# Sigmoid attention into a Swish MLP: v of the first heads loaded earlier, their values between the first score passes, and layer one's first pass dealt anew

## The chip, the cores and the metric

One core of a Trainium2 chip. The metric is the device time of one execution in microseconds. PE is the matmul engine, ACT the scalar engine (here: sigmoids and a few copies), DVE the vector engine (transpositions, casts, products), POOL the engine that issues the loads of inputs, SP the one that issues the first two loads and the stores.

## The reference

```python
scores = scale * np.matmul(q, k.transpose(0, 1, 3, 2)) - np.log(S)   # q, k, v: (8, 12, 448, 64)
attn = 1.0 / (1.0 + np.exp(-scores))
x = np.matmul(attn, v)          # then transposed to (8 * 448, 12 * 64) = (3584, 768)
h = x @ w_in                    # (768, 2048)
g = h * (1.0 / (1.0 + np.exp(-beta * h)))
out = g @ w_out                 # (2048, 768)
```

The attention is a sigmoid for each score, with no normalisation over a row, so scores and values of any piece can be worked on by themselves.

## The kernel before

**Groups and slots.** The 12 heads of a batch are three groups of four heads (g = 0, 1, 2 for batch 0; 3, 4, 5 for batch 1). A group has two slots of two heads. The 448 keys are three blocks of 128 and a last block of 64; the values `vs[b]` hold, for each of 128 partitions and each head, the three full blocks and one place for the last block, which `double_v_last` (step `E`) copies to the upper partitions.

**Loads.** q and k of a group come in one raw tile, turned by DVE into `qT` and `kT` (`transpose`, step `R`: `R3.1` makes kT of group 3, with two instructions, `R3.0` its qT). POOL issues all loads but the first two in the order of the program, with a cast from f32 to f16 on the way. The loads take turns on eight semaphores, so that a load is issued when the one eight before it has landed. `load_v` makes six loads: four of the full blocks (L136) and two of the last block (L143, rows of 64 elements). w_in comes in eight chunks (L153), each of which serves two of the sixteen column blocks of layer one; group 0's q and k come through SP as f32 and are cast by DVE and ACT (L747 to L750).

**The prologue.** For batch 0 the queries are split in two halves (c0 = 0 and c0 = QH = 224). `half_visit(g, c0, second)` is one score pass: 16 matmuls (L218) into two score tiles, then two sigmoids on ACT (L230); `second` 0 takes key blocks 0 and 1, `second` 1 block 2 and the last one. There are three score tiles in the first stage and two from then on, and a score tile is free when its sigmoid has read it. `attend(g, c0, n)` multiplies a group's weights with its values (16 matmuls, L291, into two banks) and DVE casts the two results into `xT` (L300). `idle_units` are matmuls on zeros (L740), fillers. Here the order is written out by hand: six score passes of the first query half with fillers between, then values and the first passes of the second half, then layer one's first half, `first_half(n)`: n units, each six matmuls (L171), a sigmoid (L317) and a product (L320) for one column block of 224 tokens. A unit of layer one for the other 224 tokens is a step `D0.x`.

**Behind it** the list `STEPS` gives the order of the rest, from `D0` on: `V3.1` is a score pass of group 3 with key block 1 (two score tiles, two sigmoids of 896), `A` values, `O`, `I` and `U` the two layers. Each engine runs its instructions in the order in which the steps stand.

Of the kernel before, what the change touches and what calls it, by code (L numbers as in the profile page):

```python
# [8 lines left out]
FP32 = mybir.dt.float32  # L9
FP16 = mybir.dt.float16  # L10
# [3 lines left out]
def kernel(  # L14
# [10 lines left out]
    nc = tc.nc  # L25
# [3 lines left out]
    B, H, S, D = q.shape  # L29
    NTOK, DM = out.shape  # L30
    DFF = moe_w_in.shape[1]
    P = 128
    BLK = 32
    HQ = P // BLK
    NB = S // BLK
    PAIR = D // BLK
    JF = S // P
    KL = S - JF * P
    NF = JF * P // BLK
    NPAIR = H // 2  # L40
    QPB = H // HQ
# [47 lines left out]
    def bank(name: str, cols: int = S, hold=None):  # L89
        i = min((i for i in used if i not in held.values()), key=used.get)  # L90
        touch(i)
        if hold is not None:
            held[hold] = i
        pool = psum["one" if i < N_ONE else "late"]
        return pool.tile([P, cols], FP32, tag=f"one{i}", name=name)
# [33 lines left out]
    def last_base(s: int) -> int:  # L129
        return (s % 2 ^ swapped(s // 2)) * KL  # L130

    def load_v(b: int):
        vs[b] = vp.tile([P, H, JF + 1, D], FP16, tag="v16", name="v16")
        rows = v[b].rearrange("h (p c) d -> p h (c d)", c=NB)
        for i in range(HQ):
            nc.gpsimd.dma_start(  # L136
                out=vs[b][i * BLK : (i + 1) * BLK, :, 0:JF].rearrange("p h j d -> p h (j d)"),
                in_=rows[:, :, JF * i * D : JF * (i + 1) * D],
            )
        rows = v[b].rearrange("h (p c) d -> p h c d", c=NB)  # L140
        for c in range(NF, NB):
            lo = (c - NF) * BLK
            nc.gpsimd.dma_start(out=vs[b][lo : lo + BLK, :, JF], in_=rows[:, :, c])  # L143

    def double_v_last(b: int):
        nc.vector.tensor_copy(out=vs[b][KL:P, :, JF], in_=vs[b][0:KL, :, JF])
# [44 lines left out]
    def transpose(g: int, r: int, c0: int = 0, c1: int = NB):  # L191
        raw = raws[g][:, r]
        if r == 0:
            if g not in qT:
                qT[g] = qTp.tile([P, NB * BLK, PAIR], FP16, tag="qT", name="qT")
            nc.vector.transpose(
                out=in_order(g // QPB, qT[g][:, c0 * BLK : c1 * BLK]),
                in_=raw[:, c0:c1].rearrange("p c d -> p (c d)").bitcast(FP32),
            )
            return  # L200
        kT[g] = kTp.tile([P, S, PAIR], FP16, tag="kT", name="kT")
        to = kT[g].rearrange("p k e -> p (k e)").bitcast(FP32)
        frm = raw.rearrange("p c d -> p (c d)").bitcast(FP32).rearrange("p (c f) -> p c f", c=NB)
        nc.vector.transpose(  # L204
            out=to[:, 0 : JF * P].rearrange("p (j i q) -> p i j q", j=JF, i=HQ),
            in_=frm[:, 0:NF].rearrange("p (i j) f -> p i j f", j=JF),
        )
        nc.vector.transpose(
            out=to[:, JF * P :], in_=frm[:, NF:].rearrange("p c f -> p (c f)")
        )  # L210
# [45 lines left out]
    def half_visit(g: int, c0: int, second: int):  # L256
        slots = (2 * g, 2 * g + 1)
        scos = [score_tile() for _ in slots]
        plan = [(s, jt, sco, jt * QH) for jt in (0, 1) for s, sco in zip(slots, scos)]
        widths = [S, S]  # L260
        if second:
            plan = [(s, 2, sco, 0) for s, sco in zip(slots, scos)]
            plan += [(s, JF, scos[0], QH) for s in slots]
            widths = [S, QH]
        for i in range(0, len(plan), 2):
            for e in range(PAIR):
                for s, jt, sco, u0 in plan[i : i + 2]:
                    for hh in range(2):
                        score(sco, u0, s, jt, hh, e, c0, QH)
        homes = [None, None]  # L270
        if c0 == 0 and g < QPB - 1:
            home = outp.tile([P, 2 * S], FP32, tag="osb", name="early")
            home = home.bitcast(FP16).rearrange("p (x h s) -> p x h s", x=2, h=2)
            homes = [home[:, x] for x in range(2)]
        ats = {id(sco): weigh(sco, n, at) for sco, n, at in zip(scos, widths, homes)}
        for s, jt, sco, u0 in plan:
            at_tiles[s, jt, c0] = ats[id(sco)][:, :, u0 : u0 + QH]
# [329 lines left out]
    def first_half(n: int):  # L607
        for _ in range(n):
            dense1(0, todo.pop(0), 0, QH)
# [28 lines left out]
    def follow(steps):  # L638
# [9 lines left out]
                scores_done()  # L648

    STEPS = """  # L650
        R3.1 R3.0 D0.6 D0.12 R4.1 D0.14 D0.7 V3.1 R4.0 D0.13 D0.0 D0.8 V3.0 D0.3 D0.9 V3.3 D0.1
        D0.10 E1 D0.2 Q6 V3.2 D0.4 O0.0.0 D0.5 O0.0.1 O0.0.2 V4.1 O1.0.0 O0.0.3 A3 V4.0 O1.0.1 R5.1
        D0.11 D0.15 O0.0.4 R5.0 V4.2 O0.0.5 S1.1 O0.0.6 O1.0.2 O1.0.3 S1.0 O0.0.7 S2.0 O1.0.4 V4.3
        O1.0.5 A4 V5.1 O1.0.6 O0.1.0 O0.1.1 O1.1.0 S2.1 Q7 T3.1 O1.0.7 S4.0 T2.1 O0.1.2 V5.0 T3.0
# [58 lines left out]
    with tc.manual_schedule():  # L713
        raws[0] = rawp.tile([P, 2, NB, D], FP16, tag="raw", name="raw")
        wide = gt.rearrange("p a b -> p (a b)").bitcast(FP32)
        cut = NH * D
        early = [(0, 0, NH), (1, 0, NB)]
        staged = {}
        at = 0
        for r, c0, c1 in early:  # L720
            staged[r] = wide[:, at : at + (c1 - c0) * D]
            at += (c1 - c0) * D
            nc.sync.dma_start(  # L723
                out=staged[r],
                in_=(q, k)[r][0, 0:HQ].rearrange("h (p c) d -> (h p) (c d)", c=NB)[
                    :, c0 * D : c1 * D
                ],
            )
        nc.gpsimd.memset(dummy, 0.0)
        nc.scalar.activation(out=dummy, in_=dummy, func=AF.Sigmoid, bias=0.0, scale=1.0)  # L730

        still = gt[:, NDC - 1, 0:512]
        nc.vector.memset(still, 0.0)
        beta_in = sigp.tile([P, S], FP32, tag="sg", name="beta_in")[0:BLK, 0:P]
        nc.vector.memset(beta_in, 0.0)
        idle = bank("idle_ps", 512)

        def idle_units(n: int, cols: int = 512):
            for _ in range(n):
                nc.tensor.matmul(  # L740
                    idle[:, 0:cols], still[:, 0:P], still[:, 0:cols], start=True, stop=True
                )

        idle_units(10)
        idle_units(1, 256)
        raw = raws[0].rearrange("p r c d -> p r (c d)")
        nc.vector.tensor_copy(out=raw[:, 0, 0:cut], in_=staged[0])  # L747
        transpose(0, 0, 0, NH)
        nc.scalar.copy(out=raw[:, 1, cut:], in_=staged[1][:, cut:])  # L749
        nc.vector.tensor_copy(out=raw[:, 1, 0:cut], in_=staged[1][:, 0:cut])  # L750
        transpose(0, 1)
        for g in range(1, QPB):
            load_one(g, 0, 0, NH)
            load_one(g, 1)
        load_v(0)
        nc.sync.dma_start(out=beta_in[0:NDC], in_=moe_beta.rearrange("(c p) -> c p", p=P))
        for g in range(QPB - 1):
            load_one(g, 0, NH, NB)
        for c in range(WCH):
            if c == WCH // 2:  # L760
                load_one(QPB - 1, 0, NH, NB)
            load_w_in(c)
        for g in range(1, QPB):
            transpose(g, 0, 0, NH)
            transpose(g, 1)

        for g in range(QPB):
            for second in range(2):
                half_visit(g, 0, second)
                if 2 * g + second < 2 * QPB - 1:  # L770
                    idle_units(4 if g < QPB - 1 else 2)
        double_v_last(0)
        transpose(0, 0, NH, NB)
        attend(0, 0, QH)
        half_visit(0, QH, 0)
        attend(1, 0, QH)
        half_visit(0, QH, 1)
        for g in range(1, QPB - 1):
            transpose(g, 0, NH, NB)
        attend(2, 0, QH, (0,))  # L780
        attend(2, 0, QH, (1,))
        for i in range(P // BLK):
            part = slice(i * BLK, (i + 1) * BLK)
            nc.vector.transpose(out=beta_sb[part], in_=beta_in[:, part])
        load_qk(QPB)
        load_qk(QPB + 1)
        load_v(1)
        load_w_out(0, 0)
        load_w_out(1, 0)
        load_qk(QPB + 2)  # L790
        load_w_out(0, 1)
        load_w_out(1, 1)

        firsts.close()
        share_psum(ctx, seconds, 2, N_ONE, 2)
        first_half(4)
        half_visit(1, QH, 0)
        first_half(3)
        half_visit(1, QH, 1)
        transpose(2, 0, NH, NB)  # L800
        attend(0, QH, QH)
        first_half(1)
        half_visit(2, QH, 0)
        first_half(4)
        half_visit(2, QH, 1)
        attend(1, QH, QH)
        first_half(3)
        attend(2, QH, QH)
        first_half(1)
        follow(STEPS)  # L810


# [28 lines left out]
```

## Time and profile before

| | us |
|---|---|
| median of 3 runs (368.26 to 369.42) | 368.48 |
| profiled execution | 368.51 |
| its span, first to last instruction | 366.7 |
| PE busy, fillers and all | 361.6 |
| ACT busy / DVE busy | 248.7 / 271.7 |
| first score pass starts / layer one starts | 6.00 / 19.42 |

A row of a timeline gives start, length, engine, line, operation, what it writes and reads, and in brackets how long the engine sat idle before it and what ended that. Matmul rows overlap by some hundredths at their ends. The profiled execution has 1.8 us around its span. The DMA engines are busy without a break from about 3 us to about 72 us, with 177 GB/s in the mean over the first 20 us.

### The profile page before, as it was taken

To read this page: it belongs to the slowest core of one execution; us is meant where nothing else is said; L and a number is where in the kernel's file an instruction comes from. 1 tells how busy PE (TensorE), PEld (TensorE's weight loads), DVE (VectorE), ACT (ScalarE), POOL (GpSimd) and SP (SyncE) were. 2 spreads that over 40 slices of the span, in tenths; PEclk is the share of its full clock that TensorE was granted. 3 is DMA by queue.
4 is the path that set the end of the run, shared out by engine and by line. 5 is a ranking of instruction groups with operands and counts; after the bars stand their busy time and mean duration, and the time that the engine had idled before them with its cause. 6 is when DMAs were issued, how large, how long until landed. Compare 5 with 4: busy or idle time off the path is not lost.

```text
span 366.7 us, 9126 instructions
## 1 busy us (share of the span) xinstructions
PE 361.6 (99%) x3677; PEld 238.0 (65%) x3677; DVE 271.7 (74%) x521; ACT 248.7 (68%) x409; POOL 154.3 (42%) x192
## 2 busy tenths in 40 slices
PE   8999999999999999999999999999999999999996
PEld 3478754457465685557857667666856687679763
DVE  3356569889995796876778678868878667678764
ACT  4987976789765797657865579977874859226410
POOL 7834523504413873117761445841630316316610
PEclk9999999999999999999999999999999999999999
DMA  8999999930363790416919363373303030030234
GB/s 168 184 197 201 199 206 198 236 39 2 50 139 52 160 152 2 74 64 111 156 13 149 52 137 52 49 81 89 52 1 89 2 88 2 0 88 0 56 68 138
DMA packets 42698, 34.76 MB, mean 95 GB/s; under 512 B 21904, under 2 KB 39200, under 8 KB 42656
## 3 DMA queue, kind: packets, MB, share of 16 engines
q0 software_dynamic: 36688, 22.47, 44.8%
q1 hardware_dynamic: 5968, 11.71, 11.5%
q8 instruction: 29, 0.48, 0.6%
q14 instruction: 13, 0.11, 0.1%
HBM read 45.62 MB, written 11.01 MB: 154 GB/s over the span
## 4 chain that ended last, share of the span: by engine, by line
PE 93%; DMA 3%; ACT 2%; DVE 1%; SPq 0%; issue 0%; ACTq 0%; DVEq 0%
PE m_ps L171 71%; PE sco L218 12%; PE av_ps L291 9%; DMA out_dram<-osb 2%; ACT attnT L230 1%; PE idle_ps L740 1%; DMA gt<-in_k_dram 1%; DVE osb L372 0%; SPq L602 0%; ACT osb L425 0%; DVE xT L300 0%; DVE kT L204 0%; ACT raw L749 0%; ACT osb L463 0%; SPq L723 0%
## 5 line engine op out<-in xcount | busy, mean ns | idle before, releaser
L230 ACT ACTIVATE attnT<-sco 128x896 f16<-128x896 f32 (+1 forms) x163 | 139.2, 908 | 37.8 <-PE sco L218 37.1
L372 DVE TENSOR_TENSOR osb<-m_ps,osb 128x448 f32<-128x448 f32 (+2 forms) x197 | 116.3, 596 | 51.1 <-PE m_ps L171 42.0
L171 PEld LDWEIGHTS <-w_in 128*128 128x128 f16 (+1 forms) x948 | 81.0, 100 | 18.8 <-issue 11.0
L171 PE MATMUL m_ps<-xT,w_in 128*128 128x224 f16 (+3 forms) x750 | 85.5, 266 | 0.3 <-ACT attnT L230 0.2
L492 POOL TENSOR_TENSOR gt<-osb,sg 128x448 f16<-128x448 f32 x26 | 29.5, 1135 | 117.8 <-ACT sg L425 107.7
L502 POOL TENSOR_TENSOR gt<-osb,sg 128x448 f16<-128x448 f32 x52 | 58.3, 1138 | 35.1 <-ACT sg L425 33.5
L425 ACT ACTIVATE sg<-osb,beta_sb 128x224 f32<-128x224 f32 (+1 forms) x104 | 54.0, 575 | 10.3 <-DVE osb L372 10.0
L171 PEld LDWEIGHTS <-sum 128*128 128x128 f16 (+1 forms) x444 | 39.9, 99 | 27.4 <-issue 3.6
L171 PEld LDWEIGHTS <-gt 128*128 128x128 f16 (+1 forms) x474 | 36.9, 102 | 25.7 <-issue 7.5
L171 PE MATMUL m_ps<-w_out,gt 128*128 128x384 f16 (+2 forms) x350 | 52.6, 324 | 0.0
L218 PE MATMUL sco<-qT,kT 32*128 32x448 f16 (+3 forms) x864 | 51.5, 340 | 0.3 <-ACT attnT L230 0.2
L171 PEld LDWEIGHTS <-w_S 128*128 128x128 f16 (+1 forms) x486 | 43.9, 99 | 7.0 <-issue 6.0
L171 PE MATMUL m_ps<-w_out,sum 128*128 128x384 f16 (+1 forms) x228 | 40.6, 327 | 0.0
L171 PE MATMUL m_ps<-w_T,sum 128*128 128x384 f16 (+1 forms) x216 | 40.3, 326 | 0.0
L300 DVE CAST xT<-av_ps 128x448 f16<-128x448 f32 (+1 forms) x54 | 28.4, 566 | 14.2 <-PE av_ps L291 14.1
L291 PE MATMUL av_ps<-attnT,v 128*64 128x448 f16 (+3 forms) x400 | 38.2, 343 | 0.0
L171 PE MATMUL m_ps<-xs,w_S 128*128 128x224 f16 (+1 forms) x330 | 36.2, 259 | 0.0
L291 PEld LDWEIGHTS <-v 128*64 128x64 f16 (+1 forms) x432 | 20.4, 108 | 17.7 <-issue 9.8
L425 ACT ACTIVATE osb<-m_ps,beta_sb 128x224 f32<-128x224 f32 x52 | 20.4, 448 | 15.4 <-PE m_ps L171 15.1
L218 PEld LDWEIGHTS <-kT 32*128 32x128 f16 (+1 forms) x864 | 13.5, 96 | 23.1 <-issue 21.5
L320 DVE TENSOR_TENSOR gt<-m_ps,sg 128x224 f16<-128x224 f32 (+1 forms) x40 | 16.6, 434 | 12.5 <-ACT sg L317 12.2
L463 ACT COPY osb<-m_ps 128x448 f32<-128x448 f32 x26 | 13.8, 535 | 17.7 <-PE m_ps L171 15.5
(50 smaller groups left out, 303.5 us busy)
## 6 DMA issues: line engine op xcount, KB each, us to landing
out_dram<-osb SPq DMA_DIRECT2D x100, 96.0 KB, 2.4
raw<-in_k_dram POOLq DMA_DIRECT2D x23, 224.0 KB, 5.7
raw<-in_q_dram POOLq DMA_DIRECT2D x21, 224.0 KB, 4.4
v<-in_v_dram POOLq DMA_DIRECT2D x32, 144.0 KB, 7.0
w_in<-in_moe_w_in_dram POOLq DMA_DIRECT2D x8, 384.0 KB, 10.3
w_out<-in_moe_w_out_dram POOLq DMA_DIRECT2D x4, 768.0 KB, 13.1
v<-in_v_dram POOLq DMA_DIRECT2D x16, 48.0 KB, 6.4
out_dram<-osb SPq DMA_DIRECT2D x4, 192.0 KB, 2.4
```

The costliest lines, as they stand in the source:

```text
L171: nc.tensor.matmul(to[c : c + step], hidden[:, c : c + step], weights, **({} if step == P else {"tile_position": (0, c)}), **flags,)
L218: nc.tensor.matmul(sco[base : base + nk, hh, u0 : u0 + n], kT[g][lo : lo + BLK, jt * P : jt * P + nk, e], qT[g][lo : lo + BLK, c0 : c0 + n ...
L230: nc.scalar.activation(out=at[:, :, 0:n], in_=sco[:, :, 0:n], func=AF.Sigmoid, bias=NEG_LOG_S, scale=MSCALE,)
L291: nc.tensor.matmul(av[hh * D : (hh + 1) * D, 0:n], vs[b][base : base + nk, 2 * (s % NPAIR) + hh, jt], at[base : base + nk, hh, 0:n], start ...
L300: nc.vector.tensor_copy(out=xTs[b][:, s % NPAIR, c0 : c0 + n], in_=av[:, 0:n])
L320: nc.vector.tensor_tensor(out=gt[:, dc, off : off + n], in0=m1[:, 0:n], in1=sg[:, 0:n], op=ALU.mult)
L372: nc.vector.tensor_tensor(out=out, in0=in0, in1=in1, op=op)
L425: nc.scalar.activation(out=out, in_=in_, func=AF.Sigmoid, bias=0.0, scale=beta_sb[:, dc : dc + 1])
L463: nc.scalar.copy(out=oa[:, 0], in_=m)
L492: nc.gpsimd.tensor_tensor(out=gt[:, 2 * d : 2 * d + 2, off : off + QH], in0=ob[:, 0], in1=sg, op=ALU.mult)
L502: nc.gpsimd.tensor_tensor(out=gt[:, dc, off : off + S].rearrange("p (h n) -> p h n", h=2), in0=oa[:, :, j], in1=sg, op=ALU.mult,)
L740: nc.tensor.matmul(idle[:, 0:cols], still[:, 0:P], still[:, 0:cols], start=True, stop=True)
```

## The change

- `load_v` is cut in two functions. For batch 0 the last block's two loads and the four loads of heads 0 to 3 are issued behind group 1's first query half and keys and ahead of group 2's; the four loads of heads 4 to 11 follow group 2's. Batch 0 has ten loads of v instead of six.
- Group 0's keys are cast and transposed block by block: ACT casts block 1 and the last one, DVE blocks 0 and 2, and DVE turns each block by itself.
- `attend(0, 0, QH)` stands between group 2's two first passes instead of two fillers; there are 16 fillers instead of 18 from the first pass on, and 9 and a half instead of 10 and a half before it. `attend(1, 0, QH)` and `attend(2, 0, QH)` move up as well, and `attend(2, ...)` is no longer cut in two.
- `first_half` goes 2, 2, 4, 2, 4, 2 instead of 4, 3, 1, 4, 3, 1 among the passes and values of the second query half.
- In `STEPS`, `R3.1 R3.0` come behind `D0.6 D0.12`, and `D0.13` comes ahead of `V3.1`.

```diff
-    def load_v(b: int):
-        vs[b] = vp.tile([P, H, JF + 1, D], FP16, tag="v16", name="v16")
-        rows = v[b].rearrange("h (p c) d -> p h (c d)", c=NB)
+    def load_v_full(b: int, h0: int, h1: int):
+        rows = v[b, h0:h1].rearrange("h (p c) d -> p h (c d)", c=NB)
...
+    def load_v_last(b: int):
         rows = v[b].rearrange("h (p c) d -> p h c d", c=NB)
...
-        R3.1 R3.0 D0.6 D0.12 R4.1 D0.14 D0.7 V3.1 R4.0 D0.13 D0.0 D0.8 V3.0 D0.3 D0.9 V3.3 D0.1
+        D0.6 D0.12 R3.1 R3.0 D0.14 D0.7 R4.1 D0.13 V3.1 R4.0 D0.0 D0.8 V3.0 D0.3 D0.9 V3.3 D0.1
...
-        idle_units(10)
+        idle_units(9)
         idle_units(1, 256)
...
-        nc.scalar.copy(out=raw[:, 1, cut:], in_=staged[1][:, cut:])
-        nc.vector.tensor_copy(out=raw[:, 1, 0:cut], in_=staged[1][:, 0:cut])
-        transpose(0, 1)
...
+        key_cast(nc.scalar.copy, 1)
+        nc.scalar.copy(out=raw[:, 1, NF * D :], in_=staged[1][:, NF * D :])
+        key_cast(nc.vector.tensor_copy, 0)
+        key_turn(0)
+        key_turn(1)
+        key_cast(nc.vector.tensor_copy, 2)
+        key_turn(2)
+        nc.vector.transpose(out=words[:, JF * P :], in_=raw[:, 1, NF * D :].bitcast(FP32))
+        vs[0] = vp.tile([P, H, JF + 1, D], FP16, tag="v16", name="v16")
         for g in range(1, QPB):
             load_one(g, 0, 0, NH)
             load_one(g, 1)
-        load_v(0)
+            if g == 1:
+                load_v_last(0)
+                load_v_full(0, 0, HQ)
+        load_v_full(0, HQ, H)
...
-        for g in range(QPB):
-            for second in range(2):
-                half_visit(g, 0, second)
-                if 2 * g + second < 2 * QPB - 1:
-                    idle_units(4 if g < QPB - 1 else 2)
         double_v_last(0)
+        for n in range(2 * QPB):
+            half_visit(n // 2, 0, n % 2)
+            if n == 2 * QPB - 2:
+                attend(0, 0, QH)
+            else:
+                idle_units((3, 4, 4, 4, 0, 1)[n])
         transpose(0, 0, NH, NB)
-        attend(0, 0, QH)
+        attend(1, 0, QH)
         half_visit(0, QH, 0)
-        attend(1, 0, QH)
+        attend(2, 0, QH)
         half_visit(0, QH, 1)
...
-        attend(2, 0, QH, (0,))
-        attend(2, 0, QH, (1,))
...
-        first_half(4)
+        first_half(2)
         half_visit(1, QH, 0)
-        first_half(3)
+        first_half(2)
         half_visit(1, QH, 1)
-        transpose(2, 0, NH, NB)
         attend(0, QH, QH)
-        first_half(1)
-        half_visit(2, QH, 0)
+        transpose(2, 0, NH, NB)
         first_half(4)
-        half_visit(2, QH, 1)
+        half_visit(2, QH, 0)
         attend(1, QH, QH)
-        first_half(3)
+        first_half(2)
+        half_visit(2, QH, 1)
+        first_half(4)
         attend(2, QH, QH)
-        first_half(1)
+        first_half(2)
         follow(STEPS)
```

More of the change, by code (lines that the diff above doesn't have):

```diff
@@ L130, in last_base @@
         return (s % 2 ^ swapped(s // 2)) * KL
-    def load_v(b: int):
-        vs[b] = vp.tile([P, H, JF + 1, D], FP16, tag="v16", name="v16")
-        rows = v[b].rearrange("h (p c) d -> p h (c d)", c=NB)
+    def load_v_full(b: int, h0: int, h1: int):
+        rows = v[b, h0:h1].rearrange("h (p c) d -> p h (c d)", c=NB)
         for i in range(HQ):
             nc.gpsimd.dma_start(
-                out=vs[b][i * BLK : (i + 1) * BLK, :, 0:JF].rearrange("p h j d -> p h (j d)"),
+                out=vs[b][i * BLK : (i + 1) * BLK, h0:h1, 0:JF].rearrange("p h j d -> p h (j d)"),
                 in_=rows[:, :, JF * i * D : JF * (i + 1) * D],
             )
+    def load_v_last(b: int):
         rows = v[b].rearrange("h (p c) d -> p h c d", c=NB)
@@ L143, in load_v @@
             nc.gpsimd.dma_start(out=vs[b][lo : lo + BLK, :, JF], in_=rows[:, :, c])
+    def load_v(b: int):
+        vs[b] = vp.tile([P, H, JF + 1, D], FP16, tag="v16", name="v16")
+        load_v_full(b, 0, H)
+        load_v_last(b)
     def double_v_last(b: int):
@@ L735 @@
         nc.vector.memset(beta_in, 0.0)
-        idle = bank("idle_ps", 512)
         def idle_units(n: int, cols: int = 512):
+            idle = bank("idle_ps", 512)
             for _ in range(n):
@@ L748, with key_cast, key_turn @@
         transpose(0, 0, 0, NH)
-        nc.scalar.copy(out=raw[:, 1, cut:], in_=staged[1][:, cut:])
-        nc.vector.tensor_copy(out=raw[:, 1, 0:cut], in_=staged[1][:, 0:cut])
-        transpose(0, 1)
+        whole = [
+            t[:, 0 : NF * D].rearrange("p (i j d) -> p i j d", j=JF, d=D)
+            for t in (staged[1], raw[:, 1])
+        ]
+        kT[0] = kTp.tile([P, S, PAIR], FP16, tag="kT", name="kT")
+        words = kT[0].rearrange("p k e -> p (k e)").bitcast(FP32)
+        def key_cast(copy, j: int):
+            copy(out=whole[1][:, :, j], in_=whole[0][:, :, j])
+        def key_turn(j: int):
+            nc.vector.transpose(
+                out=words[:, j * P : (j + 1) * P].rearrange("p (i q) -> p i q", i=HQ),
+                in_=raws[0][:, 1, 0:NF]
+                .rearrange("p c d -> p (c d)")
+                .bitcast(FP32)
+                .rearrange("p (i j q) -> p i j q", i=HQ, j=JF)[:, :, j],
+            )
+        key_cast(nc.scalar.copy, 1)
[7 more added lines that the diff above has]
+        vs[0] = vp.tile([P, H, JF + 1, D], FP16, tag="v16", name="v16")
         for g in range(1, QPB):
@@ L795 @@
         share_psum(ctx, seconds, 2, N_ONE, 2)
-        first_half(4)
-        half_visit(1, QH, 0)
-        first_half(3)
-        half_visit(1, QH, 1)
-        transpose(2, 0, NH, NB)
-        attend(0, QH, QH)
-        first_half(1)
+        first_half(2)
+        half_visit(1, QH, 0)
+        first_half(2)
+        half_visit(1, QH, 1)
+        attend(0, QH, QH)
+        transpose(2, 0, NH, NB)
+        first_half(4)
         half_visit(2, QH, 0)
+        attend(1, QH, QH)
+        first_half(2)
+        half_visit(2, QH, 1)
         first_half(4)
-        half_visit(2, QH, 1)
-        attend(1, QH, QH)
-        first_half(3)
         attend(2, QH, QH)
-        first_half(1)
+        first_half(2)
         follow(STEPS)
```

## The prediction

> **What bounds the kernel now.** I read the page first (busy shares, the slices, the chain), then PE's timeline of the first 45 us, then ACT's and DVE's beside it, last the DMA issues with their landings.
>
> ```profile
> PE 361.6 (99%) x3677; PEld 238.0 (65%) x3677; DVE 271.7 (74%) x521; ACT 248.7 (68%) x409; POOL 154.3 (42%) x192
> ...
> PEclk9999999999999999999999999999999999999999
> ...
> PE 93%; DMA 3%; ACT 2%; DVE 1%; SPq 0%; issue 0%; ACTq 0%; DVEq 0%
> ```
>
> PE is busy 361.6 of 366.7 us, at full granted clock, and the chain of waits is PE's own row for 93%. So a change gains only where PE waits or runs fillers, and it loses wherever it makes PE wait. PE's timeline shows where that can be:
>
> ```profile
> 1.19 4.66 PE L740 MATMUL idle_ps<-gt 128*128 128x512 f16 x11 [1.19 <-DVE gt L733]
> 6.00 0.62 PE L218 MATMUL sco<-qT,kT 32*128 32x224 f16 x16
> ...
> 14.05 0.69 PE L218 MATMUL sco<-qT,kT 32*128 32x224 f16 x14 [0.18 <-ACT attnT L230]
> ...
> 19.42 2.46 PE L171 MATMUL m_ps<-xT,w_in 128*128 128x224 f16 x24 [0.21 <-ACT attnT L230]
> 21.81 0.58 PE L218 MATMUL sco<-qT,kT 32*128 32x224 f16 x16
> 22.32 1.90 PE L171 MATMUL m_ps<-xT,w_in 128*128 128x224 f16 x18
> 24.15 0.74 PE L218 MATMUL sco<-qT,kT 32*128 32x224 f16 x16
> ...
> 33.68 3.05 PE L171 MATMUL m_ps<-xT,w_in 128*128 128x224 f16 x30
> 36.66 0.58 PE L218 MATMUL sco<-qT,kT 32*128 32x448 f16 x8
> 37.17 1.90 PE L171 MATMUL m_ps<-xT,w_in 128*128 128x224 f16 x18
> 39.00 0.62 PE L218 MATMUL sco<-qT,kT 32*128 32x448 f16 x8
> ```
>
> Until 19.42 PE waits (for ACT) or runs fillers (L740); from 19.42 on no row of PE shows a wait for another engine that lasts. ACT beside it:
>
> ```profile
> 4.76 0.56 ACT L749 CAST raw<-gt 128x448 f16<-128x448 f32 x1 [2.53 <-DMA gt<-in_k_dram]
> 6.66 6.28 ACT L230 ACTIVATE early<-sco 128x896 f16<-128x896 f32 x8 [1.33 <-PE sco L218]
> 13.08 6.29 ACT L230 ACTIVATE attnT<-sco 128x896 f16<-128x896 f32 x8
> ...
> 37.27 1.73 ACT L230 ACTIVATE attnT<-sco 128x896 f16<-128x896 f32 x2
> ```
>
> Sixteen sigmoids in a row, 6.66 to 19.37, set the first stage; layer one starts 0.05 behind the last. The pair at 37.27 shows the pace that rules the second stage: a score pass starts at 36.66, its two sigmoids end at 39.00, and the next pass starts at 39.00, since both score tiles are in use until then. So two passes cannot start closer than 2.34 us. The same stands at 21.81, whose pair ends at 24.15, when the next pass starts. The old order has just enough in between: three units of layer one, 2.34 us with the first pass.
>
> **The change, part by part**, against the profiled execution's 368.51 us (span 366.7 and 1.8 around it; the median of the runs is 368.48). A move of PE in the prologue is a move of the end, as nothing behind has slack to give.
>
> **Group 0's keys in three pieces.** Now: ACT's cast 4.76 to 5.33, DVE's transposition 5.36 to 5.94, PE at 6.00, first sigmoid 0.66 later. New: DVE's first piece still waits for ACT's first (so the built order has it). No row has these sizes. ACT's 256 columns lie between 0.32 (in proportion to 0.56 for 448) and 0.56: I take 0.40. A transposition of 128 words lies between 0.20 (64) and 0.37 to 0.41 (224): 0.28. So 5.17, first piece 5.48, second 5.68, PE at 5.54, first sigmoid at 6.20 instead of 6.66: -0.46, with -0.3 and -0.6 as bounds. The two fillers fewer (0.24 each) give nothing: they stand in the time in which PE waits for ACT anyhow.
>
> **Values between the visits.** The last pass before them, half_visit(2, 0, 0), starts at 12.43 now, at 11.97 with the head start. Then PE has in series: that pass to 12.60, attend(0) 0.92 (14.67 to 15.59 now) to 13.52, the next pass (0.62 from the release of its second tile, 14.05 to 14.67 now) to 14.2, one filler with its switch 0.31 to 14.5, attend(1) to 15.4, half_visit(0, QH, 0), whose first sigmoid can start 0.62 later, at 16.05. Kept in full, the head start would have it at 16.29 - 0.46 = 15.83; 0.22 is lost, as PE is now what is late. attend(2) follows and waits for attend(1)'s casts (second cast 1.0 behind attend(1)'s last matmuls, as at 15.4 to 16.4 now), the last pass starts at 17.1, its sigmoids at 17.9 and end at 19.25, layer one at 19.3 against 19.42: **-0.1**. Bounds: -0.46 (all kept) and +0.4 (next paragraph).
>
> **Loads.** POOL may issue a load only when the one eight before it has landed. Group 2's keys, fourth before (issued 3.03, landed 9.1), become tenth and wait for group 1's keys, landed 7.5. Ahead of them come 0.30 MB more, at 180 GB/s 1.6 us: 10.7; with a later issue up to 11.5. Add DVE's 0.58: 11.3 to 12.1, needed at 11.97. So zero, or up to 0.4. Among the bytes ahead are the 128-byte rows of v's last block; in the slices that carry them now (11.1 to 12.9) the queue still moves 166 to 202 GB/s against 172 to 192 before. [...] The other eight heads land by 12.9 to 13.7, needed at 14.5; w_in's order and total bytes ahead are the same, so its landings stay (first 16.5, last 31.5).
>
> **Layer one dealt anew.** From its start to D0.6 the old row takes 19.42 to 34.26 = 14.85 (the row at 33.68 begins with the sixteenth unit, 0.58). New, with 0.575 a unit and 0.1 a switch: 2 units 1.24; pass 0.51; 2 units 1.26; then a pass that must wait: 2.34 after its forerunner, with 0.51 + 1.26 filled, so 0.57 idle and 0.05 for the release, then 0.62; attend 0.92; 4 units 2.41; pass 0.51; attend 0.92; 2 units 1.26; pass 0.63; 4 units 2.41; attend 0.92; 2 units 1.16. Together 15.38: **+0.54**. On the gain side nothing stands: the old row has no wait for w_in (the sixth chunk lands at 27.55 and is used at 28.2, the last at 31.5 and used at 32.2). All new uses come later than landing too.
>
> **R3 behind D0.6 and D0.12, D0.13 ahead of V3.1.** DVE now does group 3's transpositions early:
>
> ```profile
> 34.46 2.75 ACT L317 ACTIVATE sg<-m_ps,beta_sb 128x224 f32<-128x224 f32 x5 [1.15 <-DVE xT L300]
> ...
> 35.25 0.57 DVE L204 STREAM_TRANSPOSE kT<-raw 128x384 f32<-128x384 f32 x1
> 35.74 0.20 DVE L208 STREAM_TRANSPOSE kT<-raw 128x64 f32<-128x64 f32 x1
> 35.87 0.60 DVE L196 STREAM_TRANSPOSE qT<-raw 128x448 f32<-128x448 f32 x1
> ```
>
> The five sigmoids stand 0.575 apart, the third (D0.12) ends 1.80 after D0.6's start (34.26). New: DVE's product for D0.12 starts at +1.83, R3.1 at +2.14, R3.0 ends 1.22 later, at +3.36, V3.1 starts at +3.42. PE has five units to do first, 2.97. Wait: **+0.45**. Then only two units (D0.0, D0.8) lie between V3.1 and V3.0 instead of three: 2.34 needed, 1.77 filled, **+0.55**. Behind V3.0 the order is the old one, and V3.3 follows two units later as before.
>
> **Sum**: -0.1 + 0.54 + 0.45 + 0.55 = +1.44; 368.51 + 1.44 = 369.95, 369.9 for a median 0.03 lower.
>
> **Rivals.** *The head start is kept in full* (not slower): if the first layer-one unit starts at 18.96, PE being ready at half_visit(0, QH, 0) by 15.2 for its sigmoid at 15.83, the sum is 0.36 less: 369.6, within 0.3%, which is 1.1 us, about what a measurement of this kernel tells from no change. If the waits also come out a quarter smaller, 369.2. For it: ACT has no idle in the stage. Against: PE's series above. Even so the end cannot be earlier than before: sixteen sigmoids from 6.20 take 12.7 us, to 18.9, and break-even needs 17.9. *PE binds before 19, not ACT*: then two fillers and the head start count whole, -0.94, and the later waits vanish: 367.6; ACT's two rows speak against it. *Group 2's keys are late*: from a landing at 11.4 on, each microsecond costs one; at 12.2 it is +0.8: 370.7. The queue's depth decides, which the trace has not shown in this order. *PE's clock falls back*: new PE stands idle some 1.4 us ahead of layer one. The first fillers take 0.42 each (11 in 4.66), those from 6.55 0.24, so a slow state exists at the start; a fall-back with as long a ramp, 4.66 at half pace, would cost about 2: 372. [...] *The change does not split v*: the built order has attend(0) wait for the first four heads' loads and the last block alone, so I give this nothing.
>
> **How the numbers follow.** Forecast 0.62 (369.9); head start kept 0.23; PE binds 0.03; late keys 0.10; clock 0.02. Slower by over 0.3%: the forecast, late keys and the clock, 0.74; within: 0.23; faster: 0.03. The range, 368.9 to 370.9, holds the kept head start with smaller waits below (369.2, and 0.3 for PE's two later gaps, 0.24 each at 179.8 and 181.2, which a moved schedule can change), and late keys above (370.7 and 0.2).
>
> **What would show it.** In the new trace: first score pass at 5.5, sigmoid at 6.2; layer one at about 19.3; a wait for ACT of about 0.6 before half_visit(1, QH, 1); V3.1 released by DVE's qT, V3.0 by ACT, both some half a microsecond late; then the old rows, all 1.4 later. Wrong: layer one before 18.6, no wait at V3.1 or V3.0, or a stretch behind 45 us in which the shift falls.

## The result, and the profile after

| | before | after |
|---|---|---|
| median of six runs each, us | 368.66 | 372.12 |
| ratio, with its 95% interval | | 1.0082 (1.0059 to 1.0105) |
| the profiled execution / its span | 368.51 / 366.7 | 373.33 / 371.2 |

The changed kernel is slower by about 3.5, where 1.4 was forecast. (The ratio is taken over all runs, not of the two medians, which alone would give 1.0094, inside the interval.) The profiled execution is the longest of the six, 1.2 above their median, so its terms are larger than what the median has to explain. Its page, the same lines as before:

```profile
PE 362.0 (98%) x3674; PEld 238.3 (64%) x3674; DVE 272.5 (73%) x524; ACT 249.4 (67%) x410; POOL 156.3 (42%) x196
...
PEclk9989999999999999999999999999999999999999
...
PE 85%; DMA 6%; DVE 3%; SPq 2%; ACT 1%; issue 1%; POOL 1%; DVEq 0%; ACTq 0%; POOLq 0%
```

PE's busy time is nearly that of before (362.0 and 361.6), while the span is 4.5 longer: PE's idle time grows from 5.1 to 9.2. Busy time hides two things that nearly cancel: the fillers take about 1.5 less, and at a granted clock of 0.50, from 21.07 to 24.48, PE is busy for 5.45 from layer one's start to the next values, where it takes 3.89 at full clock in the run with more fillers below. One digit of the granted clock is no longer 9, and the chain that ended last now runs for 6% through DMA, of which loads of v and of k have 2% each. PE's timeline, start and length first, the idle time ahead of a row in brackets:

```profile
5.30 0.58 PE L224 MATMUL sco<-qT,kT 32*128 32x224 f16 x16 [0.52 <-DVE kT L766]
...
12.67 0.58 PE L224 MATMUL sco<-qT,kT 32*128 32x224 f16 x16 [0.91 <-DVE kT L210]
...
16.04 0.99 PE L297 MATMUL av_ps<-early,v 128*64 128x224 f16 x16 [0.78 <-DMA v<-in_v_dram]
...
20.79 2.16 PE L177 MATMUL m_ps<-xT,w_in 128*128 128x224 f16 x12 [1.46 <-ACT attnT L236]
...
40.91 0.58 PE L224 MATMUL sco<-qT,kT 32*128 32x448 f16 x8 [0.38 <-DVE qT L202]
...
43.29 0.57 PE L224 MATMUL sco<-qT,kT 32*128 32x448 f16 x6 [0.25 <-ACT attnT L236]
...
45.05 0.59 PE L224 MATMUL sco<-qT,kT 32*64 32x448 f16 x8
```

And ACT's first sigmoids:

```profile
5.92 6.28 ACT L236 ACTIVATE early<-sco 128x896 f16<-128x896 f32 x8 [0.81 <-PE sco L224]
13.28 3.06 ACT L236 ACTIVATE attnT<-sco 128x896 f16<-128x896 f32 x4 [1.09 <-PE sco L224]
17.57 3.16 ACT L236 ACTIVATE attnT<-sco 128x896 f16<-128x896 f32 x4 [1.22 <-PE sco L224]
```

The first pass is early, as forecast, and V3.1 and V3.0 wait as forecast. New are a wait for group 2's keys at 12.67 and one for v's other heads at 16.04; each becomes a hole in ACT's sixteen sigmoids, which stood without a gap before. And from 20.79 twelve matmuls take 2.16 where half of the 24 in 2.46 would take 1.23.

The last row, V3.3, is a mark: from it to the end of the span all thirteen profiles of this case have 325.4 to 326.4. The shift at the mark (40.86 before, 45.05 after) adds up so:

| stretch | forecast | profile of after |
|---|---|---|
| start of layer one, 19.42 to 20.79 | -0.1 | +1.37 |
| from there to D0.6, 14.85 to 16.70 | +0.54 | +1.85 |
| D0.6 to V3.3, 6.60 to 7.56 | +1.00 | +0.96 |
| sum | +1.44 | +4.18 |

So two things are to be explained: a late start of layer one, and 1.3 too much behind it. POOL's issues show the first:

```profile
3.75 2.23 POOL L135 DMA_DIRECT2D v<-in_v_dram  x4
6.42 0.55 POOL L115 DMA_DIRECT2D raw<-in_q_dram  x1 [0.44 <-DMA raw<-in_q_dram]
7.93 0.55 POOL L115 DMA_DIRECT2D raw<-in_k_dram  x1 [0.95 <-DMA raw<-in_k_dram]
8.46 2.32 POOL L135 DMA_DIRECT2D v<-in_v_dram  x4
```

Group 2's keys (7.93) wait for the landing of group 1's keys (7.64), and land at 12.01; v's other heads land at 12.28, 15.10, 15.43 and 15.90, w_in's first chunk at 18.84 (16.51 before). What the queue moved in the meantime, in slices of 0.25 from 8 to 18, the changed kernel first and then the kernel before:

```profile
DMA  9994497479999999999999999999999999999999
GB/s 111 182 186 65 61 93 72 86 129 208 191 162 172 144 111 123 123 123 199 143 136 142 164 189 169 152 172 163 159 166 169 176 181 195 168 178 180 182 184 182
```

```profile
DMA  9999999999999999999999999999999999999999
GB/s 149 186 170 177 181 181 180 183 181 181 189 187 184 173 165 172 178 186 199 188 234 180 172 186 191 186 199 197 193 186 178 182 191 184 190 182 154 156 158 176
```

From 8.75 to 10 the queue nearly runs dry, at 61 to 93 GB/s: the six loads of v issued before 6 carry 48 KB each and have all landed by 9.02, and between 6 and 8.46 POOL issued only two loads more, as each waited for a landing. Afterwards v's packets of 384 bytes go at 333 to 340 in a microsecond (11 to 13), where before they went at 473 to 481 (9 to 11).

### The profile page after: what moved, and what is told of

Its sections match the earlier page's. It is cut to its first block, busy times and chain, and to the rows that moved or that the text cites. A ratio compares the mean times of both kernels' runs of the same rounds, so it can differ in the third digit from the quotient of the medians.

```text
span 371.2 us, 9131 instructions
## 1 busy us (share of the span) xinstructions
PE 362.0 (98%) x3674; PEld 238.3 (64%) x3674; DVE 272.5 (73%) x524; ACT 249.4 (67%) x410; POOL 156.3 (42%) x196
## 3 DMA queue, kind: packets, MB, share of 16 engines
q1 hardware_dynamic: 5968, 11.71, 11.5%
## 4 chain that ended last, share of the span: by engine, by line
PE 85%; DMA 6%; DVE 3%; SPq 2%; ACT 1%; issue 1%; POOL 1%; DVEq 0%; ACTq 0%; POOLq 0%
PE m_ps L177 66%; PE sco L224 10%; PE av_ps L297 9%; DMA out_dram<-osb 3%; DMA v<-in_v_dram 2%; DMA raw<-in_k_dram 2%; SPq L608 2%; DVE osb L378 1%; ACT attnT L236 1%; POOL v L135 0%; POOL raw L115 0%; DVE qT L202 0%; DVE kT L210 0%; ACT osb L431 0%; DVE sum L378 0%
## 5 line engine op out<-in xcount | busy, mean ns | idle before, releaser
L177 PE MATMUL m_ps<-xT,w_in 128*128 128x224 f16 (+3 forms) x750 | 86.7, 268 | 1.5 <-ACT attnT L236 1.5
L224 PEld LDWEIGHTS <-kT 32*128 32x128 f16 (+1 forms) x864 | 13.5, 96 | 25.0 <-issue 20.6
L135 POOL DMA_DIRECT2D v<-in_v_dram x36 | 21.9, 617 | 12.9 <-DMA w_out<-in_moe_w_out_dram 6.4
```

The lines of the kernel that those rows point to most:

```text
L135: nc.gpsimd.dma_start(out=vs[b][i * BLK : (i + 1) * BLK, h0:h1, 0:JF].rearrange("p h j d -> p h (j d)"), in_=rows[:, :, JF * i * D : JF * ...
L177: nc.tensor.matmul(to[c : c + step], hidden[:, c : c + step], weights, **({} if step == P else {"tile_position": (0, c)}), **flags,)
L224: nc.tensor.matmul(sco[base : base + nk, hh, u0 : u0 + n], kT[g][lo : lo + BLK, jt * P : jt * P + nk, e], qT[g][lo : lo + BLK, c0 : c0 + n ...
```

## The experiments

The times are medians; the kernel before is 368.80 beside the first four, 368.73 beside the next four and 368.37 beside the last three.

**Group 2's keys ahead of v**, still ten loads of v:

```diff
-            if g == 1:
-                load_v_last(0)
-                load_v_full(0, 0, HQ)
+        load_v_last(0)
+        load_v_full(0, 0, HQ)
         load_v_full(0, HQ, H)
```

> The changed kernel with one edit: the loads of group 2's queries and keys are issued ahead of all ten loads of v, instead of behind the six that carry v's first four heads and its last block. Theory A (the order of the loads delays group 2's keys, which landed at 12.01 in the changed kernel, and with them layer one, which began at 20.79): keys of group 2 land by about 9.5, v's first four heads by about 11.5, the other eight by about 14 to 15; layer one begins at 19.3 to 20, and the time is 0.8 to 1.5 us below the changed kernel's, 370.6 to 371.3. Rival (it is the number of loads, ten for v instead of six at 0.54 to 0.62 of POOL each, whatever their order): the keys come early, but v's other heads still land at 15.5 to 16, attend(1) waits for them, layer one begins at 20.5 or later, and w_in's first chunk lands at 18.8 as in the changed kernel; time within 0.4 of the changed kernel's.

372.20, ratio 1.0094 (1.0072 to 1.0116). The keys land at 9.28 and their pass is on time, but v's last load lands at 16.59, attend(1) waits for it, layer one starts at 22.50 (here with a fall of the clock at 17.85) and w_in's first chunk lands at 19.54:

```profile
16.73 0.99 PE L297 MATMUL av_ps<-early,v 128*64 128x224 f16 x16 [1.75 <-DMA v<-in_v_dram]
```

The rival holds: the order of the loads alone is not it. Of v's four last loads, which are equal, three had landed by 12.94.

**The old orders of layer one**, on the changed loads and early stage: `first_half` 4, 3, 1, 4, 3, 1 and the first line of `STEPS` as before.

> The changed kernel with the kernel before's order of the first passes of layer one (4,3,1,4,3,1 units between the score passes) and its written order of steps (R3 ahead of D0.6, V3.1 ahead of D0.13); loads and the early stage stay the changed kernel's. Theory B (the new orders cost 0.54 + 0.45 + 0.55 = 1.54 by themselves): D0.6 comes 0.5 earlier than the changed kernel's 37.49, V3.1 about 3.0 behind D0.6 instead of 3.42, V3.0 at once, and the time is about 1.5 below the changed kernel's: 370.4 to 370.8. Rival (the late w_in, whose sixth chunk lands at 29.61 instead of 27.55, makes the old order wait; then the new order was dealt to fit it and costs nothing here): a unit of layer one waits for DMA in the old order, and the time is within 0.5 of the changed kernel's, 371.6 to 372.6.

370.69, ratio 1.0054 (1.0033 to 1.0076). Both are partly right. The wait for w_in is there:

```profile
26.04 0.75 PE L177 MATMUL m_ps<-xT,w_in 128*128 128x224 f16 x6 [1.83 <-DMA w_in<-in_moe_w_in_dram]
```

From layer one's start (19.72) to V3.3 (43.35) it takes 23.63, which is more than the new orders take at full clock (23.05, next experiment). So the new deal does fit the late w_in; but w_in is late only because of the new loads. Of the 1.70 that this profile is ahead of the changed kernel's at V3.3, 1.07 is the start of layer one: v's last load landed at 14.10, though its loads are the changed kernel's. So that the time meets theory B's 370.4 to 370.8 is in part luck. This is also the one profile in which the early stage ran as forecast: with the loads in time for a first sigmoid at 6.61, layer one began 13.11 later, forecast 13.10.

**More fillers ahead of layer one**:

```diff
         half_visit(0, QH, 1)
+        idle_units(6)
```

> The changed kernel with six fillers of 512 columns more on TensorE, behind the last score pass ahead of layer one (half_visit(0, QH, 1)), where TensorE waits for the values' weights. Nothing else is changed. Theory C (TensorE's clock was half of full from 21.07 to 24.48 because TensorE stood idle in the microseconds before; it costs 1.2): the clock stays full in every run, layer one begins within 0.2 of the changed kernel's 20.8, the first 12 matmuls take 1.24 instead of 2.16, and the time is 0.6 (the mean over runs with and without the fall) to 1.2 lower: 370.9 to 371.5. Rival (the fall has another cause, load on the whole chip for instance, or costs nothing): the fall is seen again, or the time is within 0.3 of the changed kernel's.

371.36, ratio 1.0082 (1.0052 to 1.0111). The profile is at full clock: layer one at 20.14, its first twelve matmuls in 1.31, V3.3 at 43.19, so 23.05 for the new orders without a fall; the kernel before takes 21.44. One of six runs, 374.08, had a mean granted clock of 0.995 all the same, against three of six of the changed kernel. Layer one starts 0.65 earlier than in the changed kernel's profile, where I expected no change: the loads are the same, but v's last one lands at 15.12 instead of 15.90. The fillers are not shown to help.

**The new first line of `STEPS` alone**, on the kernel before:

```diff
-        R3.1 R3.0 D0.6 D0.12 R4.1 D0.14 D0.7 V3.1 R4.0 D0.13 D0.0 D0.8 V3.0 D0.3 D0.9 V3.3 D0.1
+        D0.6 D0.12 R3.1 R3.0 D0.14 D0.7 R4.1 D0.13 V3.1 R4.0 D0.0 D0.8 V3.0 D0.3 D0.9 V3.3 D0.1
```

> The kernel before with one edit: the first line of its written order of steps is the changed kernel's (D0.6 and D0.12 ahead of R3.1 and R3.0, D0.13 ahead of V3.1). Loads, early stage and the order of layer one's first passes stay. By the prediction V3.1 starts 3.42 behind D0.6 with a wait for VectorE's queries (+0.45), V3.0 2.34 behind it (+0.55), and the time is 1.0 above the kernel before's. Rival (these waits are taken up later, where the next steps have slack): both waits are seen, but the time is within 0.3 of the kernel before's.

369.18, ratio 1.0010 (0.9998 to 1.0022). Both waits are seen:

```profile
37.94 0.57 PE L218 MATMUL sco<-qT,kT 32*128 32x448 f16 x8 [0.37 <-DVE qT L196]
...
40.32 0.57 PE L218 MATMUL sco<-qT,kT 32*128 32x448 f16 x6 [0.25 <-ACT attnT L230]
```

V3.3 is 22.60 behind layer one's start instead of 21.44, of which 0.2 is a unit that waited for w_in. The profiled span is 1.0 longer than before's, the medians differ by 0.4; the interval reaches to 0.8, so the median lies between the 1.0 expected and the rival's 0.3. The waits are certain, their whole price in the median is not.

**v in six loads behind group 2's keys**, the rest as changed:

```diff
-            if g == 1:
-                load_v_last(0)
-                load_v_full(0, 0, HQ)
-        load_v_full(0, HQ, H)
+        load_v_last(0)
+        load_v_full(0, 0, H)
```

> The changed kernel with group 0's v in six loads (its last block in two, then all twelve heads in four) behind group 2's queries and keys, so the kernel before's number and sizes of loads; the early values, both orders of layer one and the keys in pieces stay. It differs from the kernel with group 2's keys ahead of v (ten loads, v's last at 16.59, w_in's first chunk at 19.54) only in four heads and eight heads being loaded together. Theory A2 (the small loads starve the queue: only eight are in flight, POOL needs 0.55 to 0.62 for each, and 48 KB in that time is too little): v's last load lands at 13.5 to 14.5, w_in's first chunk at about 16.5 to 17, attend(0) waits for all of v until 14 and layer one begins at 19.6 to 20.2, then 23.05 less the start from there to V3.3 as without a fall of the clock: time about 369.0 to 370.0 against 372.2 with ten loads. Rival (the early place of the values, not the loads, is what is late): layer one begins at 20.7 or later, and the time stays at 371.5 or more.

370.73, ratio 1.0065 (1.0043 to 1.0086), against 372.20 with the same order in ten loads. v's last load lands at 13.08 instead of 16.59, w_in's first chunk at 16.44 instead of 19.54, v's packets go at 492 in the microsecond from 10 to 11, and layer one starts at 19.82, inside what theory A2 gave (v came in 0.4 earlier than its 13.5). V3.3 comes 23.05 later, at 42.87, 2.0 behind the kernel before; the 369 to 370 that I expected was a slip in adding, since 2.0 on 368.7 is 370.7.

**The ten loads alone**, on the kernel before, in the changed kernel's places:

> The kernel before with one edit: group 0's v in the changed kernel's ten loads and their places (last block and first four heads ahead of group 2, the other eight heads behind it). The values stay behind all six first visits, layer one's orders stay. Theory A2: group 2's keys land at about 12.0 and its first pass starts at 12.7 instead of 12.43; w_in's chunks land some 2 later than before (first 18 to 19), so the old order of layer one's first units waits for w_in by 1 to 2 (as measured with the old order in the changed kernel: 1.83); the time is 1.5 to 2.5 above the kernel before's. Rival (these loads do harm only with early values that need them): layer one begins within 0.3 of the kernel before's 19.42, no wait for w_in, time within 0.5 of the kernel before's.

370.66, ratio 1.0056 (1.0036 to 1.0075). w_in's first chunk lands at 18.23 and the old order waits for it (0.66 at 24.48 in the profile, whose span is one of the two shortest of this kernel's six). The medians are 1.9 apart, the profiled spans 1.1. The loads alone do harm, without any early values; here group 2's keys (11.44, where I expected 12.0) still came in time, and layer one starts at 19.51, as before.

**The keys in pieces alone**, on the kernel before, with one filler less ahead (the casts and transpositions by block that the change shows):

> The kernel before with one edit: group 0's keys are cast and transposed in three pieces, as in the changed kernel, with one filler less ahead of them. By the prediction's rows the first sigmoid starts 0.46 earlier behind the landing of the keys, and, as ACT's sixteen sigmoids set this stage, layer one starts about 0.46 earlier: 18.9 to 19.0, time 0.3 to 0.5 below the kernel before's. Rival (the head start is lost at group 2's keys, which land at 9.15 and are turned on VectorE by about 12.4, or at another wait of the stage): layer one starts within 0.1 of 19.42 and the time is the kernel before's.

368.64, ratio 1.0000 (0.9986 to 1.0013). Layer one starts at 18.89:

```profile
6.13 6.28 ACT L230 ACTIVATE early<-sco 128x896 f16<-128x896 f32 x8 [1.00 <-PE sco L218]
12.56 6.28 ACT L230 ACTIVATE attnT<-sco 128x896 f16<-128x896 f32 x8
```

The sixteen sigmoids stay unbroken, 12.76 from the first to layer one's start as before. Of the 0.53 gained, 0.23 is an earlier landing of group 0's keys in this execution (4.50 against 4.73), 0.30 the pieces. That layer one met the expected 18.9 is in part luck, and the medians don't show the gain.

**The new deal of `first_half` alone**, on the kernel before:

> The kernel before with one edit: the changed kernel's order between the score passes of layer one's first units (2,2,4,2,4,2 units instead of 4,3,1,4,3,1). By the prediction half_visit(1, QH, 1) waits about 0.6 for ACT, the stretch from layer one's start to D0.6 takes 15.4 instead of 14.85, and the time is 0.54 above the kernel before's (0.3 to 0.7). Rival (the new order is free, since it also spares a wait later on): stretch within 0.15 of 14.85 and time within 0.2.

369.52, ratio 1.0021 (1.0009 to 1.0034): +0.79. Layer one's start to D0.6 takes 15.50 (19.15 to 34.65), +0.65, and V3.3 stands 22.10 behind the start, +0.66. The stretch is as expected, the time just above the expected 0.7.

**The early stage alone**: pieces and early values, with v in six loads behind group 2's keys and the old orders.

> The changed kernel's early stage alone (keys in pieces, attend(0) and attend(1) between the visits) on the kernel before's number of loads (v in six, last block first, behind group 2's keys) and its two orders of layer one. Read so far: with these loads and the new orders layer one began at 19.82 and V3.3 23.05 behind it; in the kernel before V3.3 stands 21.44 behind layer one's start. Theory (the terms add): layer one at 19.6 to 19.9, no wait for w_in, V3.3 21.4 to 21.5 behind it, time 0.2 to 0.6 above the kernel before's. Rival (the early values gain once the loads are in time, as the change is meant): layer one at 19.2 or earlier and the time below the kernel before's.

369.50, ratio 1.0036 (1.0018 to 1.0053). Layer one at 19.71, V3.3 21.45 behind it: the terms add. With the same keys in pieces and the values behind all passes, layer one had started at 18.89. The early values cost 0.8 even with the better loads. Layer one starts 13.68 behind the first sigmoid, against 12.76 without them. Of these 0.92, 0.35 is PE's series, which the run with the old orders also shows (13.11); for the rest, v lands at 12.97, attend(0) starts at 13.07 and holds back the pass behind it, for which ACT waits 0.56. The median is 1.1 above the kernel before's, where 0.2 to 0.6 was expected; half of its eight runs had a mean clock under 0.999.

**Six loads and the fillers**, to look at the clock again:

> The kernel with v in six loads (new orders, early values) with six fillers of 512 columns more behind half_visit(0, QH, 1), where TensorE waits 1.46 for ScalarE ahead of layer one. Read so far: the granted clock changes only at whole multiples of 3.41 from the moment at which it became full (4.00 to 21.07 is five of them, in the kernel with group 2's keys first 4.19 to 17.85 is four), and fell after stretches with TensorE busy 1.95 and 1.67 of 3.41. Theory C2 (a stretch of 3.41 with TensorE busy for little more than half halves the clock for the next): with the hole filled the clock is 1.0 (0.998 or more) in all six runs, and the time is that of the six-load kernel's runs at full clock, 370.2 to 371.0. Rival (the fall has nothing to do with this hole): a run with 0.995 again, as in one of six there.

370.71, ratio 1.0076 (1.0048 to 1.0104). Five runs lie at 370.1 to 371.3, and one, with a clock of 0.995, at 373.55. The rival holds: filling that one hole does not end the falls.

**No fillers among the first passes**, on the kernel before:

```diff
                 half_visit(g, 0, second)
-                if 2 * g + second < 2 * QPB - 1:
-                    idle_units(4 if g < QPB - 1 else 2)
```

> The kernel before without the fillers between the first six score passes (18 matmuls of 512 columns), so TensorE does 0.6 of work in each 1.6 there. Theory C2: the clock, once full, halves at the end of a 3.41 stretch within these visits although TensorE never stands idle for 3.41, the longest idle stretch being about 1.0; passes take 1.0 instead of 0.6 to 0.7. ScalarE sets the stage, so layer one starts at most 0.5 later, and if the clock is not full again by then, its first 24 matmuls take up to 4.9 instead of 2.46: time 0.3 to 3 above the kernel before's. Rival (the clock falls only when TensorE is idle for a whole 3.41): it stays full and the time is within 0.3.

372.02 (371.68 to 372.32, four runs), ratio 1.0101 (1.0086 to 1.0115), all of them with a clock of 0.981 to 0.986. Stretches of 3.41 from the moment at which the clock became full, in this kernel and then in the changed one; the columns are the stretch, its length, PE's busy time with its matmuls, the granted clock, the DMA share and GB/s:

```profile
4.54:7.96 3.42, 1.41 (x22) 1.00 1.08 163
7.96:11.37 3.41, 2.31 (x32) 0.50 1.50 177
...
14.78:18.20 3.42, 2.59 (x34) 0.50 1.36 179
18.20:21.61 3.41, 3.41 (x52) 0.50 1.40 186
21.61:25.02 3.41, 3.19 (x43) 1.00 1.42 196
```

```profile
14.24:17.65 3.41, 2.63 (x51) 1.00 1.29 172
17.65:21.07 3.42, 1.95 (x35) 1.00 1.37 167
21.07:24.48 3.41, 3.41 (x32) 0.50 1.42 196
24.48:27.89 3.41, 3.40 (x50) 1.00 1.45 198
```

In these two profiles the clock halved at the end of a stretch in which PE was busy for 1.41 and for 1.95, although without the fillers it never stood idle for longer than 1.17 in one piece there, and was full again behind one with 3.41; 2.17 to 2.59 of 3.41 at half clock did not bring it back. One stretch of the kernel with v in six loads was busy for as long as the one ahead of the changed kernel's fall, and the clock stayed full behind it:

```profile
17.40:20.81 3.41, 1.95 (x34) 1.00 1.35 179
20.81:24.22 3.41, 3.06 (x52) 1.00 1.42 200
```

So if the busy time decides, the limit lies near 1.95 of 3.41, an estimate from these stretches. The longest idle time in one piece does not sort the stretches: it was 1.17, 1.75 and 1.46 ahead of the three falls in the profiles, and 1.46 and 1.23 to 1.26 in the four least busy stretches without one. The stretches are counted from the moment at which the clock became full, 4.00 to 7.16 in the profiles; that this decides which runs of one kernel have a fall is not shown.

Since the passes then take 0.94 to 1.37 and hold up ACT, layer one starts at 23.27 instead of 19.42, of which 0.40 is a later first sigmoid (7.06). The rival, an idle time of a whole 3.41, is ruled out, and the falls fit theory C2; its price does not: I allowed 0.5 for layer one's start and at most 3 in all, and the time is 3.65 above.

## Why the prediction was wrong

**The loads are the step that failed**, and with them the start of layer one, put at 19.3 (-0.1) and found at 20.79 (+1.37). The text named what decided here, that a load is issued when the one eight before it has landed (group 2's keys at 7.93, behind a landing at 7.64), and then priced bytes: 0.30 MB ahead of group 2's keys at 180 GB/s, landing 10.7 to 11.5. But with eight in flight and 48 KB in most of them the queue was not kept at 180 GB/s, and while POOL waited for group 1's keys it ran nearly dry (61 to 93). Measured: keys 12.01, the other heads 15.90 (forecast 12.9 to 13.7). By the early stage's own row (last pass of the first half 5.77 behind the first sigmoid, layer one 13.10 behind it, both met in the run with the old orders) the late keys cost 0.98 and the late heads 0.79. The bound for late keys was also mis-stated: its own terms, a landing at 11.5 and 0.58 for DVE against 11.97, give 0.1, not 0.4. And the reading of the slices with v's 128-byte rows looked at the queue's rate alone; in the kernel before's profile a packet of 128 bytes took 32 ns in the median and one of 384 bytes, three times the data, 51.

**"Its landings stay" was the same mistake** for w_in. Over all profiles, v's last load lands at 14.05 to 16.59 in the five kernels with ten loads of v and at 12.97 to 14.06 in the eight with six; w_in's first chunk at 18.23 to 19.54 against 16.33 to 17.12. "The old row has no wait for w_in" was true only with the old landings, and only just: with the new loads the old order waits 0.66 to 1.83, and with the old loads a unit waited 0.2 in one profile.

**Two rivals came in on top of the forecast, not in its place.** Late keys had 0.10 and +0.8, and cost about that. The fall of the clock had 0.02 and about +2: it costs 1.20 in the profile (1.85 in the stretch to D0.6, less the 0.65 that the deal takes by itself), and the three runs of the changed kernel at 0.995 lie 1.2 above the three at full clock (372.7 and 371.5 in the mean). I gave it so little because the one idle time of 1.4 that I foresaw seemed too short; no run shows how long an idle time a fall would take. What the runs show is falls behind stretches of 3.41 with PE busy for 1.41 to 1.95 and idle for 1.17 to 1.75 in one piece at most; that the busy share decides, with the limit near 1.95, is an estimate.

**What held.** The new deal +0.65 (forecast 0.54). V3.1 3.42 behind D0.6 and V3.0 2.38 behind it (3.42 and 2.34), together +0.96 (1.00). The head start came to 0.48 in the changed kernel (first sigmoid 1.44 behind the keys' landing, 1.92 before; forecast 0.46) and to 0.30 alone. That 0.48 is the best of a spread: in the eight profiles with the keys in pieces the first sigmoid stands 1.44 to 1.88 behind the landing, in the five without 1.87 to 1.97. It was also right that the head start could not be kept as a gain with the values in series: alone they cost 0.8. The sign followed from these terms, the size did not.

So the shift at V3.3 is -0.12 (19.30 for 19.42, the start as forecast) - 0.28 (first sigmoid at 5.92 for 6.20, as group 0's keys landed earlier in this execution) + 0.98 + 0.79 + 0.65 + 1.20 + 0.96 = 4.18. That is the one profile. Over the runs, the three at full clock are 2.8 above the kernel before's median; if the two orders cost their 1.6 in each of them, about 1.2 is left for the loads and the values, and the falls add 0.6 in the mean. This split is an estimate.

**What stays open.** Why v's packets go at two thirds of the former pace even when the queue has been refilled, and why the last of v's loads lands up to 3.7 behind its forerunner, isn't shown; no run took the loads' size and number apart, nor the eight in flight from POOL's 0.54 to 0.62 for each load. Nor is it known where the clock fell in the two executions at 0.995 with extra fillers, as only one execution of each kernel has a trace, and those were not it. No version here beats the kernel before; the pieces alone equal it.

## What to carry to other kernels

Price a moved or split load by what it leaves in flight, not by bytes alone: here a load went out only behind the landing of the one eight before it, six loads of 48 KB ahead of group 2's keys left the queue at 61 to 93 GB/s from 8.75 to 10, and w_in's eight chunks, further behind, landed 1.8 to 2.5 later than before. When a stage is paced by one engine's unbroken row, work put between its suppliers must fit the gap and have its operands there, or it breaks the row, as here, where ACT stood idle for 1.09 and 1.22 in it. And before fillers are removed or exchanged for real work that can wait, add up the matmul engine's busy time in stretches, not its longest gap alone: the three falls of the clock in these profiles came behind stretches of 3.41 with 1.41 to 1.95 busy, and their longest gaps were 1.17 to 1.75.

## What the runs showed of the hardware

In the three profiles with a fall, the granted clock went from full to 0.50 and back at whole multiples of 3.41 behind the moment at which it first became full: 4.00 to 21.07 and 24.48 in the changed kernel, 4.54 to 7.96 and 21.61 without fillers, 4.19 to 17.85 and 21.26 with the keys ahead of v. It halved behind stretches with PE busy for 1.95, 1.41 and 1.67, in this order, and stayed full behind 2.03 (the old orders on the changed loads), 2.15 (the early stage alone) and 2.17 (the keys ahead of v). One stretch of 1.95, in the six-load kernel, was not followed by a fall, so a limit there, 57% of the stretch, is an estimate, or the falls rest on something that these rows don't show.
